# Where the x tiles begin in a partition, and when the first sum of w_out's blocks takes its temporaries

## The chip, the core and the metric

The kernel runs on one core of a Trainium2 chip. The metric is the time of one execution on the device, in microseconds (us), as the median of several runs. TensorE (PE) does the matrix products, VectorE (DVE), ScalarE (ACT) and GpSimd (POOL) the work between them, and SyncE (SP) issues the transfers (DMA). Each engine takes its instructions in a fixed order and waits, where it must, with all that is queued behind.

## What is computed

Attention with a window of keys and block summaries, then a feed-forward layer whose activation is the square of relu:

```python
def _attn_ref(q, k, v):                       # (4, 8, 768, 64) each
    block, window = (32, 16)
    k_sum = k.reshape(B, H, nb, block, D).max(axis=3)
    v_sum = v.reshape(B, H, nb, block, D).mean(axis=3)
    scores_l = scale * np.matmul(q, k.transpose(0, 1, 3, 2))
    mask_l = np.abs(pos[:, None] - pos[None, :]) < window
    scores_s = scale * np.einsum('bhsd,bhnd->bhsn', q, k_sum) + np.log(block)
    scores_all = np.concatenate([np.where(mask_l, scores_l, -1e9), scores_s], axis=-1)
    a = softmax(scores_all)
    return np.matmul(a, np.concatenate([v, v_sum], axis=2))

def _moe_ref(x, w_in, w_out):                 # x: 3072 x 512, the attention's result
    h = x @ w_in                              # 512 x 2048
    g = np.maximum(h, 0.0) ** 2
    return g @ w_out                          # 2048 x 512
```

## The kernel before

**Tiling.** The 3072 tokens are six units of 512. A group is 64 tokens; eight groups make a unit. For each group the kernel forms scores against 118 keys (94 of the window and 24 blocks), a softmax, and the values, and writes the result x into two SBUF tiles: `xh`, x rounded to the engine's fast 32-bit type, and `xl`, the rest. Both are rings of two units (16 groups x 64 tokens x 4 slices of 128). Weights and activations are split in the same way, and each product is made of three terms (high by high, high by low, low by high).

**Products.** `FI{u}_{f}` is the first product of unit u with block f of w_in (16 blocks): 12 matmuls of 128x512, eight that stream `xh` and four that stream `xl`, on L1018 for units 0 and 1 and on L1305 for the later ones. `FO{u}_{f}` is the second product, 12 matmuls on L1042 that stream w_out. For the last four units the second products are taken on sums of blocks (a two-level scheme that spares products): L1419 has 112 groups of six matmuls (`FP`), that stream sums of w_out's blocks; a mixed stage near 440 to 522 us does a part of the first products in the same way (`SP0`, `SP1`, ..., L1610), with sums of x in `xs`, `xgh`, `xgl`, `xa`, or in `xkb`, which are parts of the tile `kb` that is free by then.

**Weights.** Block f of w_in and of w_out comes as 64-bit words (`WL0_f` and `WL1_f`, two loads of 512 KB on SP, L952). It is converted by a chain over two engines: ACT forms `t` from `raw` (`WM`, L955), DVE shifts `raw` (`WR`, L958) and joins the two (`WJ`, L964), ACT rounds to the high part of `w` (`WH`, L969), DVE forms the low part (`WW`, L972). `t` is one of three temporaries, which the sums below take too.

**Sums of w_out's blocks.** `combine(p)` adds two blocks of w_out on POOL (`RC`, L1111, and `SC`, L1126), rounds on ACT (`SH`, L1129), forms the rest on DVE (`SL`, L1132), and stores sums (`WS`) and plain blocks (`WA`, L1144, three transfers of 256 KB) in DRAM, from where they are fetched for the later products.

**Values.** The probabilities of a group are transposed by a turn through DRAM: `TW` stores them (four transfers of 64 KB, L826), `TR` fetches them (256 KB, L832). The visit `V{g}` on PE is the scores of two later groups (L638) and then the values of the groups g-1 and g (L842), which wait for `TR`.

**Order.** A planner in the kernel sets the order on each engine before anything is built. Every task has a due time, worked out from constants (`Q_LEAD`, `AT_FIRST`, `KEEPS`, `PRODUCT_STEP` and others), a modelled duration, and lists of what it waits for and what buffers it takes (`take`) and uses (`use`); `behind` names a task that must have begun before. The planner gives an engine the ready task with the earliest due time.

**Addresses.** Constant tiles (`cst.tile`) lie one behind the other in each partition, in the order in which they are made. `LINE` is 256 bytes. `scratch` and the three `nm` tiles are 64 bytes each; before, none of them lies ahead of `xh`, and in the program as built `xh` begins 1664 bytes into the partition, `xl` at 18048 and `kb` at 47488: each 128 bytes past a multiple of 256. The tiles of weights, activations and sums other than `xkb` begin at multiples of 256.

Of the kernel before, what the change touches and what calls it, by code (L numbers as in the profile page):

```python
# [10 lines left out]
F32 = mybir.dt.float32  # L11
# [9 lines left out]
P = 128  # L21
# [5 lines left out]
LINE = 256  # L27
# [3 lines left out]
TU = UG * TQ  # L31
# [18 lines left out]
FV_LEAD = 0  # L50
FV1_LEAD = 17.0
HALVED = 2
Q_LEAD = 23
XS_LEAD = 7
R_LEAD = 1
TR_LEAD = 18
WITH_ITEM = 0, 0, 1, 1, 0, 1, 0, 0, 0, 1, 0, 0, 1, 1, 1, 1
AT_FIRST = 3
LATER = 22
EARLIER = 12  # L60
X_LEAD = 0
KEEPS = 20
GH_LEAD = 9


# [172 lines left out]
def attention_then_relu2_ffn(  # L238
# [13 lines left out]
    NT, DM = out.shape  # L252
# [14 lines left out]
    cst = ctx.enter_context(tc.tile_pool(name="cst", bufs=1))  # L267
# [4 lines left out]
    add = plan.add  # L272

    kinds = {}
# [3 lines left out]
    def const(shape, name, dtype=F32):  # L278
        cols = -(-4 * math.prod(shape[1:]) // LINE) * LINE // 4
        return cst.tile([shape[0], cols], dtype, name=name)[:, : math.prod(shape[1:])]  # L280
# [54 lines left out]
    MIXED_STEP = 1.66  # L335
    X_BY = 40
    SUMS = 231.1, 245.7, 260.4, 275.0
    PRODUCT_STEP = 1.48, 1.58, 1.40
    A0, A1, B0, B1 = 12.0, 2.0, 21.0, 2.2
    HALF_AT = 25.0, 32.0  # L340
    MX = 0.95
# [1 line left out]
    unit_at, products_at, at = [], [], T0  # L343
# [31 lines left out]


    ident = cst.tile([P, P], F32, name="ident")
    kb = sb.tile([P, NPAIR, NB + S], F32, tag="kb", name="kb", bufs=1)
    xh = cst.tile([P, KT, RING * TQ], F32R, name="xh")
    xl = cst.tile([P, KT, RING * TQ], F32R, name="xl")  # L380
# [34 lines left out]
            )  # L415


    scratch = cst.tile([P, LINE // 16], F32, name="scratch")
    kinds["nm"] = Slots(None, "nm", 3, [cst.tile([P, LINE // 16], F32, name=f"nm{i}") for i in range(3)])

    def table():
        nc.scalar.activation(scratch[:, :1], unscale[:, :1], AF.Exp)
# [25 lines left out]
    for g in reversed(range(NG)):  # L448
        pairs = (P, NPAIR, P)
# [32 lines left out]
    vs_bufs = {}  # L482

    means = const([P, S // P * NB], "means")

    def make_means():

# [200 lines left out]
    def softmax(g, by_pe=False):  # L688
# [104 lines left out]
        if wide:  # L793
            at_ps = h_buf(f"t{g}")

            def turn():
                for p in range(NPAIR):
                    nc.tensor.transpose(
                        out=at_ps.tile[:, p * P : (p + 1) * P], in_=pr.tile[:, p, :], identity=ident
                    )  # L800

            t_T[g] = add(f"T{g}", "PE", 0.5, turn, due - 9, [t_n, t_ident], take=[at_ps], use=[pr])

            def turned():
                nc.scalar.copy(
                    out=a.tile.rearrange("k (i n r) -> k n i r", i=NSQ, n=NPAIR),
                    in_=at_ps.tile.rearrange("k (n i r) -> k n i r", n=NPAIR, i=NSQ),
                )

            t_A[g] = add(f"A{g}", "ACT", 0.47, turned, due - 8.5, [t_T[g]], take=[] if early else [a], use=[at_ps] + [a] * early)  # L810
        else:


            def turn():
                nc.vector.transpose(
                    out=a.tile.rearrange("p (j n r) -> p j n r", j=NSQ, n=NPAIR),
                    in_=pr.tile.rearrange("p n (j c) -> p j n c", c=SQ),
                )

            assert not early  # L820
            t_T[g] = add(f"T{g}", "DVE", 0.63, turn, due - 9, [t_n], take=[a], use=[pr])
            d = buf("turn", 4, (NSQ, SQ, NSQ, NPAIR * SQ), F32, f"turn{g}", dr)

            def store():
                for i in range(NSQ):
                    nc.sync.dma_start(  # L826
                        out=d.tile[:, :, i, :].rearrange("j c e -> c j e"),
                        in_=a.tile[i * SQ : (i + 1) * SQ].rearrange("c (j e) -> c j e", j=NSQ),
                    )

            def fetch():
                nc.sync.dma_start(out=a.tile, in_=d.tile.rearrange("j c i e -> (j c) (i e)"))  # L832

            t_w = add(f"TW{g}", "SP", 1.75, store, due - 8.5 - TR_LEAD, [t_T[g]], take=[d], use=[a], size=4 * P * DM)
            t_A[g] = add(f"TR{g}", "SP", 0.35, fetch, due - 8 - TR_LEAD, [t_w], use=[a, d], size=4 * P * DM)

    def values(both, x_of):
        for i, g in enumerate(both):
# [78 lines left out]


    t_W = {}
    w_parts = {}  # L920

    def convert(f, ns):

# [53 lines left out]
        for i in range(k):  # L977
# [2 lines left out]
                behind=t1[0] if i else None, size=P * 4096, begin=due - 31,  # L980
            ))
        t2 = add(f"WM{name}", "ACT", 0.02 + 0.5 * k, rebias, due - 8, t1, take=[t], use=[raw])
        t3 = add(f"WR{name}", "DVE", 0.09 + 0.27 * k, rest, due - 8, t1, use=[raw])
        t4 = add(f"WJ{name}", "DVE", 0.03 + 0.54 * k, join, due - 7, [t2, t3], use=[raw, t])
        t6 = add(f"WH{name}", "ACT", 0.08 + 0.43 * k, high, due - 6, [t4], take=[w], use=[t])
# [116 lines left out]

    def combine(p):

        due = unit_at[0] + 75 + 13.5 * p + LATER * (p > 5)
        ws = [w_parts[1, 2 * p + k] for k in range(2)]
        raw = buf("t", 3, (P, 2 * DM), F32, f"cr{p}")
        sums = buf("t", 3, (P, 2 * DM), F32, f"cs{p}")
# [38 lines left out]
        for k in range(2):  # L1147
            t1.append(add(
                f"RC{p}_{k}", "POOL", 1.3, lambda k=k: whole(k), due + 1.3 * k, t_W[1, 2 * p + k],
                take=[raw, sums] * (not k), use=[raw] * k + ws[k], begin=due, behind=t1[0] if k else None,  # L1150
            ))
        t2 = add(f"SC{p}", "POOL", 2.9, add_up, due + 2.6, t1, use=[raw, sums])
        t3 = add(f"SH{p}", "ACT", 0.97, high, due + 6, [t2], use=[raw, sums])
# [308 lines left out]
    def sum_x():  # L1462
# [10 lines left out]
            tag: [buf(tag, n, (P, DM), F32R, f"x{tag}{k}") for k in range(2)] for tag, n in (("a", 2), ("gl", 3), ("gh", 3))  # L1473
        }

        def halves(x, k0=0):
            return [Part(x, (2 * k0 + k) * TU, (2 * k0 + k + 1) * TU) for k in range(2)]

        homes = {
            3: (halves(of_kb), halves(of_kb, 1)), 0: (halves(of_kb, 2), pairs["a"]), 2: (halves(slots[0]), pairs["gl"]),  # L1480
            1: (halves(slots[1]), pairs["gh"]),
        }
        takes = {
# [373 lines left out]
```

## Time and profile before

| what | us |
|---|---|
| timed runs | 599.33, 600.30, 601.23 |
| median of the runs | 600.3 |
| the profiled execution | 604.56 |
| span of its trace | 602.7 |
| PE busy in the span | 585.3 (97%) |
| DVE busy | 415.9 (69%) |
| ACT busy | 342.2 (57%) |
| POOL busy | 96.6 (16%) |

The span runs from the first to the last instruction of the profiled execution; 1.9 us of that execution lie around it. The profiled execution is 4.26 us longer than the median of the timed runs. Starts in a timeline are microseconds from the span's start. Matmuls are pipelined: a matmul's own duration reaches over the start of the next, so that the pace of PE is read from start to start.

### The profile page before, as it was taken

How to read it: one execution, taken by the hardware profiler on the slowest of the kernel's cores; microseconds unless marked ns; L12 is line 12 of the kernel's file. 1: busy time of each engine (PE TensorE's matmuls, PEld its weight loads, DVE VectorE, ACT ScalarE, POOL GpSimd, SP SyncE). 2: the span in 40 equal slices, each digit the busy share in tenths (PEclk: the TensorE clock that was granted, in tenths of full speed). 3: DMA queues.
4: the chain of work that ended last, by engine and by line, in shares of the span. 5: the costliest groups of instructions: out<-in, count | busy, mean ns of one | idle time of the engine just before them, and what ended most of it. 6: DMA issues, size and time to landing. Idle time of an engine off the chain costs nothing.

```text
span 602.7 us, 11842 instructions
## 1 busy us (share of the span) xinstructions
PE 585.3 (97%) x4108; PEld 473.5 (79%) x4108; DVE 415.9 (69%) x942; ACT 342.2 (57%) x848; POOL 96.6 (16%) x141
## 2 busy tenths in 40 slices
PE   8889999989999999999989999999999999999996
PEld 6678878768887888888877888888888878788885
DVE  5999897666544615655975867798754945678764
ACT  2899687566654535564864566645643544454442
POOL 4400005263450016264300000000000000000000
PEclk9999999989999999999999999999999999999999
DMA  8999964977994757966998765878976144567672
GB/s 312 294 386 327 346 247 156 299 253 234 380 326 152 237 197 230 358 221 231 283 306 283 227 185 179 278 226 239 312 216 191 35 145 151 161 194 226 193 228 100
DMA packets 100958, 143.83 MB, mean 239 GB/s; under 512 B 10060, under 2 KB 55116, under 8 KB 100900
## 3 DMA queue, kind: packets, MB, share of 16 engines
q1 hardware_dynamic: 100900, 143.09, 73.3%
q8 instruction: 32, 0.52, 0.4%
q14 instruction: 26, 0.21, 0.1%
HBM read 102.42 MB, written 39.85 MB: 236 GB/s over the span
## 4 chain that ended last, share of the span: by engine, by line
PE 82%; DMA 7%; DVE 5%; ACT 2%; issue 2%; SPq 1%; DVEq 0%
PE o L1419 25%; PE h L1305 22%; PE o L1042 10%; PE h L1018 9%; PE o L1610 4%; PE x L842 3%; PE att L638 2%; DMA a<-turn 2%; PE sz L1610 2%; PE o L638 1%; DVE t L964 1%; DMA q<-qW 1%; DMA kb<-kT 1%; PE att L1610 1%; DMA v<-vS 1%
## 5 line engine op out<-in xcount | busy, mean ns | idle before, releaser
L1419 PE MATMUL o<-gh,w 128*128 128x512 f32 x448 | 121.0, 391 | 0.0
L1401 ACT CAST gh<-g 128x512 fp32r<-128x512 f32 x112 | 68.5, 621 | 60.9 <-PE o L1419 29.2
L1305 PE MATMUL h<-xh,w 128*128 128x512 f32 x320 | 100.7, 396 | 0.0
L1419 PEld LDWEIGHTS o<-gh,w 128*128 128x128 f32 x448 | 83.6, 188 | 17.8
L1406 DVE TENSOR_TENSOR gl<-g,gh 128x512 fp32r<-128x512 f32 x112 | 77.7, 706 | 24.0 <-ACT gh L1401 23.3
L1018 PE MATMUL h<-xh,w 128*128 128x512 f32 x240 | 76.9, 400 | 1.7 <-DVE w L972 1.0
L1305 PEld LDWEIGHTS h<-xh,w 128*128 128x128 f32 x320 | 59.8, 188 | 14.1
L1315 ACT ACTIVATE r<-h 128x512 f32<-128x512 f32 x48 | 28.5, 596 | 73.8 <-PE h L1305 72.9
L1419 PE MATMUL o<-gl,w 128*128 128x512 f32 x224 | 69.2, 389 | 0.0
L1305 PE MATMUL h<-xl,w 128*128 128x512 f32 x160 | 63.2, 395 | 0.0
L767 ACT ACTIVATE p<-p,nm 128x118 f32<-128x118 f32 x160 | 61.2, 388 | 2.5 <-DVE nm L712 2.5
L1042 PE MATMUL o<-w,gh 128*128 128x512 f32 x240 | 62.5, 396 | 0.0
L1018 PEld LDWEIGHTS h<-xh,w 128*128 128x128 f32 x240 | 45.3, 190 | 13.3 <-DVE w L972 1.7
L1042 PEld LDWEIGHTS o<-w,gh 128*128 128x128 f32 x240 | 44.9, 190 | 10.4
L1419 PEld LDWEIGHTS o<-gl,w 128*128 128x128 f32 x224 | 42.0, 188 | 9.0
L1018 PE MATMUL h<-xl,w 128*128 128x512 f32 x120 | 47.9, 400 | 0.0
L1032 DVE TENSOR_TENSOR gl<-r,gh 128x512 fp32r<-128x512 f32 x30 | 22.9, 764 | 33.6 <-PE o L1042 21.8
L712 DVE CUSTOM_DVE_ANT_0 p<-att,mask 128x118 f32<-128x118 f32 x152 | 32.9, 274 | 13.6 <-PE att L638 13.5
L651 POOL COPY kb<-kb 128x96 f32<-128x96 f32 x25 | 11.0, 440 | 181.2 <-ACT kw L663 60.4
L1111 POOL TENSOR_TENSOR cr<-w 128x512 f32<-128x512 f32 x16 | 26.4, 1666 | 73.3 <-PE vps L539 41.5
L1027 ACT ACTIVATE r<-h 128x512 f32<-128x512 f32 x30 | 17.9, 597 | 32.5 <-PE h L1018 32.5
L1305 PEld LDWEIGHTS h<-xl,w 128*128 128x128 f32 x160 | 30.1, 188 | 7.2
(200 smaller groups left out, 998.4 us busy)
## 6 DMA issues: line engine op xcount, KB each, us to landing
raw<-wW SPq DMA_DIRECT2D x32, 512.0 KB, 7.6
w<-scr_s SPq DMA_DIRECT2D x64, 256.0 KB, 2.8
w<-scr_a SPq DMA_DIRECT2D x48, 256.0 KB, 3.3
turn<-a SPq DMA_DIRECT2D x160, 64.0 KB, 2.6
a<-turn SPq DMA_DIRECT2D x40, 256.0 KB, 4.7
w<-scr_i SPq DMA_DIRECT2D x40, 256.0 KB, 5.5
v<-vS SPq DMA_DIRECT2D x33, 192.0 KB, 6.1
kb<-kT SPq DMA_DIRECT2D x16, 384.0 KB
```

Source lines behind the costliest of these rows:

```text
L712: nc.vector.tensor_tensor_reduce(out=pr.tile[:, j, :KEYS], in0=score_at(g, 0, j), in1=mask_of(g)[0], scale=-SCALE, scalar=-NEG, op0=ALU.ad ...
L767: nc.scalar.activation(x, score_tile(g, p % parts)[:, p] if by_pe else x, AF.Exp, bias=nm.tile[:, p : p + 1], scale=SCALE if by_pe else -1 ...
L1018: nc.tensor.matmul(cut(h), lhsT=lhs.tile[:, k * P : (k + 1) * P], rhs=rhs[:, k, c0 : c0 + n], start=(i == 0), stop=(i == 3 * KT - 1),)
L1032: lambda: nc.vector.tensor_tensor(out=cut(gl), in0=cut(r), in1=cut(gh).bitcast(F32), op=ALU.subtract),
L1042: nc.tensor.matmul(o_of(o, t), lhsT=terms[i][0].tile[:, (t - t0) * P : (t - t0 + 1) * P], rhs=terms[i][1].tile, start=(first and i == 0), ...
L1111: nc.gpsimd.tensor_tensor(out=raw.tile[:, k * DM : (k + 1) * DM], in0=ws[k][0].tile.bitcast(F32), in1=ws[k][1].tile.bitcast(F32), op=ALU.add)
L1305: nc.tensor.matmul(h.tile, lhsT=lhs.tile[:, k * P : (k + 1) * P], rhs=rhs[:, k, c0 : c0 + TU], start=(i == 0), stop=(i == 3 * KT - 1),)
L1315: t2 = add(f"RL{name}", "ACT", 0.56, lambda: nc.scalar.activation(r.tile, h.tile, AF.Relu), due + 2 - R_LEAD, [t1], take=[r], use=[h])
L1401: f"GH{s}_{n}", "ACT", 0.54, lambda x=x, gh=gh: nc.scalar.copy(out=gh.tile, in_=x.tile), due - GH_LEAD, ready,
L1406: lambda x=x, gh=gh, gl=gl: nc.vector.tensor_tensor(out=gl.tile, in0=x.tile, in1=gh.tile.bitcast(F32), op=ALU.subtract),
L1419: nc.tensor.matmul(o.tile[:, d], lhsT=chunk.tile[:, w * HALF + d * P : w * HALF + (d + 1) * P], rhs=y.tile, start=begins and w == 0 and y ...
L1610: nc.tensor.matmul(o.tile, lhsT=lhs(w, k), rhs=y[k], start=begins and i == 0, stop=i == 5, skip_group_check=not begins,)
```

## The change

It has three parts.

1. `scratch` and one `nm` tile are made ahead of `kb`, `xh` and `xl`, and the two other `nm` tiles behind `means`. In the program as built `xh` then begins at 1792 and `xl` at 18176, both multiples of 256; masks, `v`, the probabilities `p` and `means` move by 128 bytes as well, to multiples of 256. `kb` stays at 47488, and the parts of it that hold sums of x (`xkb`) begin 128 bytes further in.
2. The first task of `combine` (`RC0_0`) gets `behind=t_WM[-1]`: it takes its temporaries once the last conversion's `WM15` has begun.
3. Constants of the planner: `Q_LEAD` 23 to 9, `AT_FIRST` 3 to 4, `KEEPS` 20 to 30, the second `PRODUCT_STEP` 1.58 to 1.59, and `combine` due 1 us later. `FETCH_LATE` is zero and has no effect.

```diff
-Q_LEAD = 23
+FETCH_LATE = 0.0
+LATE_FROM = 8
+COMB0 = 76
+COMB1 = 13.5
+Q_LEAD = 9
...
-AT_FIRST = 3
+AT_FIRST = 4
...
-KEEPS = 20
+KEEPS = 30
...
-    PRODUCT_STEP = 1.48, 1.58, 1.40
+    PRODUCT_STEP = 1.48, 1.59, 1.40
...
     ident = cst.tile([P, P], F32, name="ident")
+    scratch, *small = (cst.tile([P, LINE // 16], F32, name=f"small{i}") for i in range(2))
     kb = sb.tile([P, NPAIR, NB + S], F32, tag="kb", name="kb", bufs=1)
     xh = cst.tile([P, KT, RING * TQ], F32R, name="xh")
...
-    scratch = cst.tile([P, LINE // 16], F32, name="scratch")
-    kinds["nm"] = Slots(None, "nm", 3, [cst.tile([P, LINE // 16], F32, name=f"nm{i}") for i in range(3)])
+    kinds["nm"] = Slots(None, "nm", 3, small)
...
     means = const([P, S // P * NB], "means")
+    small += [cst.tile([P, LINE // 16], F32, name=f"small{i}") for i in range(2, 4)]
...
-    w_parts = {}
+    w_parts, t_WM = {}, []
...
         t2 = add(f"WM{name}", "ACT", 0.02 + 0.5 * k, rebias, due - 8, t1, take=[t], use=[raw])
+        t_WM.append(t2)
...
-        due = unit_at[0] + 75 + 13.5 * p + LATER * (p > 5)
+        due = unit_at[0] + COMB0 + COMB1 * p + LATER * (p > 5)
...
-                take=[raw, sums] * (not k), use=[raw] * k + ws[k], begin=due, behind=t1[0] if k else None,
+                take=[raw, sums] * (not k), use=[raw] * k + ws[k], begin=due, behind=t1[0] if k else t_WM[-1],
...
-        def halves(x, k0=0):
-            return [Part(x, (2 * k0 + k) * TU, (2 * k0 + k + 1) * TU) for k in range(2)]
+        def halves(x, k0=0, at=0):
+            return [Part(x, at + (2 * k0 + k) * TU, at + (2 * k0 + k + 1) * TU) for k in range(2)]
...
-            3: (halves(of_kb), halves(of_kb, 1)), 0: (halves(of_kb, 2), pairs["a"]), 2: (halves(slots[0]), pairs["gl"]),
+            3: (halves(of_kb, 0, LINE // 8), halves(of_kb, 1, LINE // 8)), 0: (halves(of_kb, 2, LINE // 8), pairs["a"]), 2: (halves(slots[0]), pairs["gl"]),
```

The planner's order changes with it. The names below are those of the tiles, with a running number behind; lines of the changed kernel are a few higher than those of the kernel before.

**ACT near the end of unit 0, 105 to 130 us.** `r0_10` is the activation of `FI0_10`, `t15<-raw15` is `WM15`, `w15<-t15` is `WH15`, `cr0<-cs0` is `SH0`. Before:

```order
L1027 ACTIVATE r0_10_1451<-h0_10_1425 128x512
...
L955 ACTIVATE t14_1513<-raw14_1467 128x1024
...
L1129 CAST cr0_1496<-cs0_1497 128x1024
...
L1027 ACTIVATE r0_13_1642<-h0_13_1582 128x512
L1028 ACTIVATE r0_13_1642<-r0_13_1642 128x512
L1029 CAST gh0_13_1666<-r0_13_1642 128x512
L955 ACTIVATE t15_1673<-raw15_1423 128x1024
L1027 ACTIVATE r0_14_1696<-h0_14_1653 128x512
L969 CAST w15_1705<-t15_1673 128x2x512
```

And now:

```order
L1033 ACTIVATE r0_10_1452<-h0_10_1426 128x512
L960 ACTIVATE t15_1468<-raw15_1406 128x1024
L1034 ACTIVATE r0_10_1452<-r0_10_1452 128x512
L1035 CAST gh0_10_1475<-r0_10_1452 128x512
L1033 ACTIVATE r0_11_1480<-h0_11_1454 128x512
L974 CAST w15_1495<-t15_1468 128x2x512
...
L960 ACTIVATE t14_1526<-raw14_1470 128x1024
...
L1135 CAST cr0_1518<-cs0_1519 128x1024
L1034 ACTIVATE r0_13_1587<-r0_13_1587 128x512
```

The conversion of block 15 moved from behind the activation of `FI0_13` to the activation of `FI0_10`, ahead of block 14. The two DVE steps of block 15 moved with it, from behind `GL0_13` to around `GL0_10`. PE's own order changes there too: from `FO0_10 FI0_12 FO0_11 V13 FI0_13 FO0_12 FI0_14 FO0_13 FI0_15` to `FI0_12 FO0_10 FI0_13 V13 FO0_11 FI0_14 FO0_12 FI0_15 FO0_13`.

**SP, 97 to 110 us.** `raw15` is loaded by `WL0_15` and `WL1_15`, `scr_a0` by `WA0`, `turn13<-a13` is `TW13` and `a13<-turn13` is `TR13`. Before:

```order
L1144 DMA scr_a0_96<-w1_0_702 256x1x256
...
L952 DMA raw15_1423<-wW 128x512
L826 DMA turn12_1439<-a12_1415 32x4x128 x4
L826 DMA turn13_1446<-a13_1444 32x4x128 x4
L952 DMA raw14_1467<-wW 128x512 x2
L952 DMA raw15_1423<-wW 128x512
L832 DMA a12_1415<-turn12_1439 128x512
L832 DMA a13_1444<-turn13_1446 128x512
```

And now:

```order
L957 DMA raw15_1406<-wW 128x512
...
L957 DMA raw15_1406<-wW 128x512
...
L1150 DMA scr_a0_96<-w1_0_702 256x1x256
L1150 DMA scr_a0_96<-w1_1_745 256x1x256 x2
L831 DMA turn12_1440<-a12_1416 32x4x128 x4
L831 DMA turn13_1447<-a13_1445 32x4x128 x4
L957 DMA raw14_1470<-wW 128x512 x2
L837 DMA a12_1416<-turn12_1440 128x512
```

Both loads of block 15 moved ahead of `WA0`; between the stores and the fetches of the turn stand now two weight loads where there were three.

**PE in the mixed stage, 486 to 492 us.** `o0` is an accumulator whose two halves `SP11` (`xkb`), `SP12` (`xs1`, `xgh`) and `SP13` (`xs0`, `xgl`) write in turn; `h5_13` is that of `FI5_13`. Before:

```order
L1610 MATMUL o0_66<-xkb_5367,w5_948 128x512 x6
L1610 MATMUL o0_66<-xs1_5433,w0_1_665 128x512 x4
L1610 MATMUL o0_66<-xgh0_5437,w0_1_665 128x512
L1610 MATMUL o0_66<-xgh1_5447,w0_1_665 128x512
L1610 MATMUL o0_66<-xs0_5407,w7_1035 128x512 x4
```

And now:

```order
L1616 MATMUL o0_66<-xkb_5367,w6_971 128x512 x6
L1616 MATMUL o0_66<-xs1_5433,w0_1_665 128x512 x4
L1616 MATMUL o0_66<-xgh0_5437,w0_1_665 128x512
L1616 MATMUL o0_66<-xgh1_5448,w0_1_665 128x512
L1311 MATMUL h5_13_5479<-xh_74,w7_1035 128x512 x2
...
L1616 MATMUL o0_66<-xs0_5407,w4_913 128x512 x4
```

`FI5_13`, which came after `SP15`, moved between `SP12` and `SP13`.

## Rows read from the trace of the kernel before

**Rows 1.** The page: busy time, share of the span, instructions of PE.

```profile
PE 585.3 (97%) x4108; PEld 473.5 (79%) x4108; DVE 415.9 (69%) x942; ACT 342.2 (57%) x848; POOL 96.6 (16%) x141
```

**Rows 2.** Waits of PE: who waits for whom; us in total, times, longest.

```profile
PE x L842 <- DMA a<-turn: 1.7, 2, 1.2
PE o L1610 <- ACT g L1628: 1.4, 2, 0.7
PE h L1018 <- DVE w L972: 1.0, 2, 0.8
PE h L1018 <- ACT w L969: 0.7, 1, 0.7
```

**Rows 3.** Groups by line and form: count | busy us, mean ns | idle before.

```profile
L1419 PE MATMUL o<-gh,w 128*128 128x512 f32 x448 | 121.0, 391 | 0.0
L1305 PE MATMUL h<-xh,w 128*128 128x512 f32 x320 | 100.7, 396 | 0.0
L1018 PE MATMUL h<-xh,w 128*128 128x512 f32 x240 | 76.9, 400 | 1.7 <-DVE w L972 1.0 <-ACT w L969 0.7
```

**Rows 4.** Timeline of PE, three places: start, us, line, operation, count, idle before.

```profile
187.06 0.62 PE L1018 MATMUL h<-xh,w 128*128 128x512 f32 x2
...
189.85 1.99 PE L1042 MATMUL o<-w,gh 128*128 128x512 f32 x8
...
192.59 0.62 PE L1018 MATMUL h<-xh,w 128*128 128x512 f32 x2
...
523.17 1.08 PE L1419 MATMUL o<-gh,w 128*128 128x512 f32 x4
...
596.63 0.61 PE L1419 MATMUL o<-gh,w 128*128 128x512 f32 x2
```

**Rows 5.** Timeline of PE in the mixed stage, two places.

```profile
480.61 1.56 PE L1610 MATMUL o<-xkb,w 128*128 128x512 f32 x6
482.01 0.40 PE L1305 MATMUL h<-xh,w 128*128 128x512 f32 x1
...
488.96 1.07 PE L1610 MATMUL o<-xs,w 128*128 128x512 f32 x4
489.87 0.61 PE L1610 MATMUL o<-xgh,w 128*128 128x512 f32 x2
```

**Rows 6.** Timeline of PE at the end of unit 0.

```profile
114.29 1.32 PE L842 MATMUL x<-a,v 118*64 118x64 f32 x32 [1.21 <-DMA a<-turn]
...
125.80 1.07 PE L1042 MATMUL o<-w,gl 128*128 128x512 f32 x4
...
135.98 0.64 PE L638 MATMUL att<-kb,q 64*64 64x118 f32 x16
```

**Rows 7.** Stretches: busy of PE, PEld, DVE, ACT, POOL; granted clock, DMA share, GB/s.

```profile
94.00:98.00 4.00, 4.00 (x19) 3.32 (x18) 3.62 (x16) 3.94 (x17) 2.69 (x4) 1.00 0.27 88
...
108.00:116.00 8.00, 6.79 (x84) 5.39 (x84) 4.00 (x5) 4.82 (x7) 0.16 (x1) 1.00 1.02 330
...
130.00:133.00 3.00, 3.00 (x9) 2.39 (x8) 1.70 (x1) 0.03 (x1) 3.00 (x3) 0.52 0.95 347
```

**Rows 8.** Timeline of SP's DMA issues at the end of unit 0.

```profile
101.34 0.51 SPq L952 DMA_DIRECT2D raw<-wW  x1
101.96 3.82 SPq L826 DMA_DIRECT2D turn<-a  x8
105.83 1.41 SPq L952 DMA_DIRECT2D raw<-wW  x3
107.28 1.08 SPq L832 DMA_DIRECT2D a<-turn  x2
...
128.25 1.14 SPq L832 DMA_DIRECT2D a<-turn  x2
```

**Rows 9.** Timeline of ACT at the end of unit 0.

```profile
110.99 1.17 ACT L955 ACTIVATE t<-raw 128x1024 f32<-128x1024 f32 x1 [5.20 <-DMA raw<-wW]
...
123.66 1.15 ACT L955 ACTIVATE t<-raw 128x1024 f32<-128x1024 f32 x1
```

More of the change, by code (lines that the diff above doesn't have):

```diff
@@ L834, in softmax @@
             t_w = add(f"TW{g}", "SP", 1.75, store, due - 8.5 - TR_LEAD, [t_T[g]], take=[d], use=[a], size=4 * P * DM)
-            t_A[g] = add(f"TR{g}", "SP", 0.35, fetch, due - 8 - TR_LEAD, [t_w], use=[a, d], size=4 * P * DM)
+            t_A[g] = add(f"TR{g}", "SP", 0.35, fetch, due - 8 - TR_LEAD, [t_w], use=[a, d], size=4 * P * DM, late=FETCH_LATE * (g >= LATE_FROM))
     def values(both, x_of):
```

## The prediction

> **What bounds the kernel now.** I read the page's busy times first: PE is busy for 585.3 of 602.7 us [rows 1]. So a saving has to come out of PE: out of its pace while it is busy, or out of its few waits. The other engines, at 69% and less, matter only where PE waits for them. Next the list of PE's waits [rows 2]: four of its entries lie, all but a part of the first, where the order is changed, and they make 4.8 us together. Third, the groups by line, for what a busy PE pays per matmul [rows 3]: those that stream `xh` (L1018, L1305) average 396 to 400 ns, the L1419 ones, of the same shape, 391. Such a duration overlaps the next, so the real pace is read from starts. `FI` at 187.06 to 189.85 makes 12 matmuls in 2.79 us, 232.5 ns each; the `FO` behind it, 189.85 to 192.59, 12 in 2.74; and from 523.17 to 596.63 lie 324 matmuls of L1419, 226.7 ns each [rows 4]. Whatever streams x is 2.6% slower per matmul than whatever streams w or sums of w.
>
> Is that the address? The mixed stage compares on one line, into the same accumulators, with the same kind of weights: six that stream `xkb`, 480.61 to 482.01, take 233 ns each; four that stream `xs`, 488.96 to 489.87, 227.5 [rows 5]. `xkb`, `xh` and `xl` begin 128 bytes past a multiple of 256, `xs` on one. What the matmul writes, and which product it is, is thus no explanation; the place of the streamed operand is, though a trace of before can't exclude another property that these three tiles share.
>
> **Part 1, the addresses.** Per matmul 232.5 - 226.7 = 5.8 ns. `FI` matmuls: L1018 has 240 with `xh` [rows 3], at eight of twelve per product 30 products; L1305 has 320 [rows 3], 40 products, and by the code eight more with weights in other tiles. That makes 78 products and 936 matmuls; the mixed stage adds 112 that stream `xh`, `xl` or `xkb`. 1048 x 5.8 ns = 6.1 us. The product behind an `FI` seems to pay a little too, 2.74 against 12 x 0.2267 = 2.72, some 15 to 20 ns; for 30 `FO`s and some 20 places in the mixed stage 0.8 us. Ceiling 6.9. Not all of it reaches the end: up to the ninth product of unit 0 PE follows the conversions on DVE, and two visits (near 200 and 324 us) wait for a transfer that doesn't start earlier; I take off 0.7. **6.2 us**, with bounds: nothing if the address is not the cause, 6.9 if all reaches the end. `v`, the weights of the 640 value products, moves to a multiple of 256 too. No row shows `v` in either place, so its price lies between nothing and, at the same 5.8 ns for each, 3.7 us; weight loads run beside matmuls here (PEld 79% busy under PE's 97% [rows 1]), so I take nothing and keep the other end for the range. Masks, `p` and `means` are operands of engines with room: nothing either way.
>
> A page speaks against this part. The Trainium skill, "SBUF — State Buffer", section "Specifications (TRN2)", gives cachelines of 16 bytes and names no larger unit; 128 and 256 are both whole numbers of them, so by that rule a shift of 128 bytes moves no matmul. Rows 5 don't agree with that being all; the case has its rival below.
>
> **Part 2, the last conversion.** `FI0_15` waits twice, for `WH15` on ACT and then `WW15` on DVE, 0.7 and 0.8 us [rows 2]. The cause is on ACT: `WM15` begins at 123.66, behind the softmax of groups 14 and 15 and `GH0_13` [rows 9], though half of its weights were asked for at 101.34 and the rest before 107.3 [rows 8]. And it costs more than the waits: from 130 to 133 us the granted clock is 0.52 [rows 7], the lower of the two levels (1.2 instead of 2.4 GHz), right behind PE's pauses. Sum by starts: from 125.80, where the last four matmuls of a product begin, to 135.98, where the next visit does, stand 4 + 12 + 12 matmuls [rows 6]; at 227, 233 and 227 ns they need 0.91 + 2.79 + 2.72 = 6.42 of the 10.18 us. 3.76 are lost; some 1.7 of that to the clock (6 matmuls of `FI0_15` and those of `FO0_14` at up to twice the time), 2.0 to the waits and to PE's refill. In the new order `WM15` stands behind the activation of `FI0_10`, some 18 us earlier, and both loads of block 15 ahead of `WA0`, so the wait goes whole: **3.7 us**, or 2.0 if the timed runs don't show the lower clock that this execution shows. The first sum gives its place up: `RC0` waits for `WM15`, and `SC0` for the temporary that `WW15` frees, on POOL, where nobody on PE waits for it; behind it on the queues stand `SH0` (ACT) and `SL0` (DVE), and behind those the softmax of groups 14 and 15. That is the rival on V15.
>
> **Part 3, V13.** It waits 1.21 us for the fetch of the turned probabilities [rows 2, 6]. The fetches are issued at 107.28, right behind three weight loads of 512 KB issued from 105.83 [rows 8], and the transfers run full from 108 to 116 us at 330 GB/s [rows 7], while from 94 to 98 us they were 0.27 busy. One of the three now goes out near 100 us: 512 KB / 330 GB/s = 1.6 us earlier landing, near 112.7. PE, by a faster x, is there near 112.4 instead of 113.1, with as many products before it as before. Wait 0.3 instead of 1.2: **0.9 us**; bounds 0 (the place is taken by other transfers) and 1.2.
>
> **Then V15.** Where a wait goes, the next need comes sooner. The fetch for V15 was issued at 128.25 to 129.4 [rows 8], and its values begin one microsecond behind 135.98 [rows 6]: ample. With part 2, part 3 and x, PE is there some 5.5 us earlier, near 131.4. The fetch hangs on DVE and ACT (softmax of groups 14, 15), which get only part of that, so it lands between 129 and 133. I take **0.7 us given back**, bounds 0 and 1.6.
>
> **Mixed stage.** `SP13` waits 0.7 us for ACT to copy half of its accumulator [rows 2], one of two waits of that kind. With `FI5_13` (2.8 us) in front the copy is covered: **0.8 us** with the refill, bounds 0 and 1.0. The second wait stands between products whose order is unchanged and stays. The other constants swap loads late in the kernel, ahead of which PE has no wait in the list; q's loads go out later, but no entry of PE's waits names them: nothing, up to 1 us lost.
>
> **Sum.** -6.2 - 3.7 - 0.9 + 0.7 - 0.8 = -10.9 us on the profiled execution of 604.56 us: 593.7. That execution is 4.26 us above the median of the timed runs; from 600.3 the same sum gives 589.4, and 591.1 without the clock's share. I set **590.0**.
>
> **The rivals.**
> (a) The address is not the cause. Then all matmuls on x stay at 233 ns, and 600.3 - 4.7 = 595.6. For it: three tiles only share an address class, and the page above. Against: rows 5, on one line. 0.10.
> (b) The address works, the end of unit 0 gives its gain back, because V15 waits for its fetch longer than I took or the clock falls behind that new pause. 600.3 - 6.2 - 0.8 - 0.9 = 592.4. For it: the fetch's chain runs over three engines and SP. Against: the wait begins only if the fetch lands after 131.4. 0.22.
> (c) Slower. `WM15` now stands on ACT in front of `SQ0_10` and `GH0_10`. If block 15's weights land late, ACT stands with all of that behind it, and so does PE at `FO0_10`. In before a load issued at 105.83 kept ACT waiting till 110.99, 5.2 us [rows 8, 9]; both loads of block 15 are issued by about 102, so by 107 they are there. PE reaches `FO0_10` some 5.6 us after `FI0_10`'s end, of which ACT and DVE need 3.6, so it loses one us for each that the weights land after 107.8, and to be over 602.1 with the rest of the sum right they must land after 120.5 (after 114.3 if (a) holds too). Time then 603 or more. Against: SP issues them ahead of `WA0`. 0.04.
> (d) The gain is larger: `v` counts too. 600.3 - 10.9 - 2 to 3.7 = 586 to 587. 0.04.
>
> **How the numbers follow.** Forecast 0.60, (a) 0.10, (b) 0.22, (c) 0.04, (d) 0.04. The range goes from 586.5 (forecast with most of what `v` could give) to 595.0 (all of (b) and the lower half of (a)); about 0.1 is left out above and little below. What a measurement of this kernel can tell from no change is about 0.3%, 1.8 us. Faster by more than that: forecast, (b), (d) and most of (a), 0.93. Within: 0.03, a mixture of (a) and a partial (c). Slower: 0.04.
>
> **What would show it.** In the changed kernel's trace: L1018's and L1305's matmuls at the pace of L1419 (12 in about 2.72 us, means near 391 ns); if they stay at 2.79, part 1 is wrong. `FI0_15` without a wait, and a granted clock of 1.00 from 130 to 134 us; else part 2. PE's wait for `a<-turn` at V13 under 0.5 us, and at V15 under 1; else part 3 or (b). One wait for L1628's copy instead of two. A wait of ACT for `raw` longer than 2 us before `WM15` would be (c). The prediction is wrong if a new wait over 2 us stands in PE's list, or if the streams of x keep their pace.

## The result and the profile after

| | before | after |
|---|---|---|
| median of seven runs each, us | 601.23 (599.27 to 604.92) | 595.08 (593.83 to 598.31) |
| the profiled execution | 604.56 | 595.08 |
| span of its trace | 602.7 | 593.0 |
| PE busy in the span | 585.3 | 577.6 |

The ratio after to before is 0.9894 (95% interval 0.986 to 0.9928): a gain of 6.2 us where 10.3 were forecast. The time lies 0.08 us above the upper end of the range; as a gain, from 600.3, the range went from 5.3 to 13.8 us, and 6.2 lies in it. The two traces differ by 9.7 us; but the profiled execution of before was 3.3 us above the median of its seven runs and that of after is its median, and 9.7 - 3.3 = 6.4.

The groups by line and form of after (count | busy us, mean ns of one | idle before), which answer to [rows 3]:

```profile
L1425 PE MATMUL o<-gh,w 128*128 128x512 f32 x448 | 120.6, 391 | 0.0
L1311 PE MATMUL h<-xh,w 128*128 128x512 f32 x320 | 99.1, 391 | 0.0
L1024 PE MATMUL h<-xh,w 128*128 128x512 f32 x240 | 74.2, 390 | 0.0
```

And the timeline of PE at the place of [rows 4]:

```profile
184.42 0.62 PE L1024 MATMUL h<-xh,w 128*128 128x512 f32 x2
...
187.14 1.98 PE L1048 MATMUL o<-w,gh 128*128 128x512 f32 x8
...
189.86 0.39 PE L1024 MATMUL h<-xh,w 128*128 128x512 f32 x1
```

The streams of x now have the mean of the others, and an `FI` takes 2.72 us, 226.7 ns a matmul, as does the `FO` behind it. Part 1 does what it says. The list of PE's waits (us in total, times, longest), against [rows 2]:

```profile
PE x L847 <- DMA a<-turn: 3.7, 3, 1.8
...
PE o L1616 <- ACT g L1634: 0.7, 1, 0.7
```

No wait of an `FI` for ACT or DVE is left in it, and one of the two waits in the mixed stage is gone; the wait for fetched probabilities has grown from 1.7 to 3.7 us. The timeline of PE shows where (in brackets the idle time before, and what ended it):

```profile
130.03 0.63 PE L643 MATMUL att<-kb,q 64*64 64x118 f32 x16
...
132.91 0.69 PE L847 MATMUL x<-a,v 118*64 118x64 f32 x16 [1.84 <-DMA a<-turn]
...
133.90 0.82 PE L847 MATMUL x<-a,v 118*64 118x64 f32 x16 [0.30 <-DMA a<-turn]
...
138.91 0.39 PE L1024 MATMUL h<-xh,w 128*128 128x512 f32 x1
```

The row at 130.03 is the start of V15, that at 138.91 the start of `FI1_0`. V13 waits no longer, V15 does, and behind that wait the clock falls: stretches of after (length, then busy of PE, PEld, DVE, ACT, POOL, granted clock, DMA share, GB/s), against [rows 7]:

```profile
126.00:130.00 4.00, 4.00 (x19) 3.05 (x17) 4.00 (x3) 1.39 (x3) 2.32 (x2) 1.00 0.54 166
130.00:134.00 4.00, 1.85 (x52) 1.52 (x53) 0.90 (x9) 0.00 (x0) 0.00 (x0) 1.00 1.03 332
134.00:138.00 4.00, 4.00 (x25) 3.20 (x24) 1.87 (x10) 3.24 (x14) 1.23 (x2) 0.57 1.08 388
```

In before it was at the lower of its two levels from 130 to 133 us, behind the pauses of `FI0_15`; now it is from 134 to 138, behind that of V15.

Where the 9.7 us arise, by the starts of tasks that both traces have:

| start of | before | after | lead of after |
|---|---|---|---|
| `FI0_10` | 98.09 | 97.12 | 0.97 |
| V13 | 112.04 | 111.14 | 0.90 |
| V15 | 135.98 | 130.03 | 5.95 |
| `FI1_0` | 140.92 | 138.91 | 2.01 |
| `FI2_0` | 234.47 | 231.21 | 3.26 |
| V31 | 302.42 | 297.96 | 4.46 |
| V35 | 345.50 | 339.66 | 5.84 |
| `SP12` | 488.96 | 481.18 | 7.78 |
| first of the last `FP` stage | 521.78 | 512.07 | 9.71 |

Between V13 and V15 the edit gains 5.05 us; between V15 and `FI1_0`, where nothing was edited, 3.94 are lost again. From the start of V15 to that of `FO0_15` it is 4.62 us in after and 2.05 in before: 2.14 of waiting, and 0.43 in which PE starts anew behind its two pauses. `FO0_15` itself takes 4.26 us instead of 2.89: 1.37 for the lower clock. After that the lead only grows.

### The profile page after: what moved, and what is told of

Read it like the earlier page. It is cut to its first block, busy times and chain, and to the rows that moved or that the text cites. A ratio compares the mean times of both kernels' runs of the same rounds, so it can differ in the third digit from the quotient of the medians.

```text
span 593.0 us, 11845 instructions
## 1 busy us (share of the span) xinstructions
PE 577.6 (97%) x4108; PEld 473.5 (80%) x4108; DVE 414.4 (70%) x942; ACT 342.2 (58%) x848; POOL 92.2 (16%) x141
## 4 chain that ended last, share of the span: by engine, by line
PE 74%; DMA 15%; DVE 4%; SPq 3%; issue 2%; ACT 1%; DVEq 0%; ACTq 0%
PE o L1425 24%; PE h L1311 22%; PE o L1048 8%; PE h L1024 7%; DMA raw<-wW 4%; PE o L1616 4%; PE x L847 3%; PE att L643 2%; DMA a<-turn 2%; PE sz L1616 2%; DMA v<-vF 1%; DMA turn<-a 1%; DMA qvpa_lent<-vF 1%; DMA kb<-kT 1%; DMA scr_a<-w 1%
## 5 line engine op out<-in xcount | busy, mean ns | idle before, releaser
L1311 PE MATMUL h<-xh,w 128*128 128x512 f32 x320 | 99.1, 391 | 0.0
L1024 PE MATMUL h<-xh,w 128*128 128x512 f32 x240 | 74.2, 390 | 0.0
L1311 PE MATMUL h<-xl,w 128*128 128x512 f32 x160 | 62.3, 389 | 0.0
L772 ACT ACTIVATE p<-p,small 128x118 f32<-128x118 f32 x160 | 61.1, 386 | 1.3 <-DVE small L717 1.3
L1024 PE MATMUL h<-xl,w 128*128 128x512 f32 x120 | 46.7, 389 | 0.0
L656 POOL COPY kb<-kb 128x96 f32<-128x96 f32 x25 | 9.5, 378 | 178.2 <-ACT kw L668 59.6
L1117 POOL TENSOR_TENSOR cr<-w 128x512 f32<-128x512 f32 x16 | 25.0, 1584 | 59.5 <-PE vps L544 40.7
```

Source lines behind the costliest of these rows:

```text
L772: nc.scalar.activation(x, score_tile(g, p % parts)[:, p] if by_pe else x, AF.Exp, bias=nm.tile[:, p : p + 1], scale=SCALE if by_pe else -1 ...
L1024: nc.tensor.matmul(cut(h), lhsT=lhs.tile[:, k * P : (k + 1) * P], rhs=rhs[:, k, c0 : c0 + n], start=(i == 0), stop=(i == 3 * KT - 1),)
L1117: nc.gpsimd.tensor_tensor(out=raw.tile[:, k * DM : (k + 1) * DM], in0=ws[k][0].tile.bitcast(F32), in1=ws[k][1].tile.bitcast(F32), op=ALU.add)
L1311: nc.tensor.matmul(h.tile, lhsT=lhs.tile[:, k * P : (k + 1) * P], rhs=rhs[:, k, c0 : c0 + TU], start=(i == 0), stop=(i == 3 * KT - 1),)
```

## The experiments

Ratios are to the kernel before on the same chip, with 95% intervals. Four runs stand first: the addresses alone, the order alone, the kernel before once more, and one fetch put ahead of a store.

**The addresses alone.** The kernel before with

```diff
+    scratch, *small = (cst.tile([P, LINE // 16], F32, name=f"small{i}") for i in range(2))
     kb = sb.tile(...)
     xh = cst.tile(...)
...
-            3: (halves(of_kb), halves(of_kb, 1)), 0: (halves(of_kb, 2), pairs["a"]), ...
+            3: (halves(of_kb, 0, LINE // 8), halves(of_kb, 1, LINE // 8)), 0: (halves(of_kb, 2, LINE // 8), pairs["a"]), ...
```

> The kernel before with the new addresses alone (xh, xl, xkb at multiples of 256; order of every engine as before). Theory A, the address sets the pace of the matmuls that stream x: 12 of an FI in 2.72 us instead of 2.79, 6 to 7 us less in all, ratio 0.988 to 0.990; the waits at V13 and FI0_15 stay or grow by what PE gains ahead of them. Rival B, the pace comes with the order or with something else of the changed kernel: FI stays at 2.79 us, ratio 1.00.

Measured: 597.26 us, ratio 0.9927 (0.9898 to 0.9955), span 595.7. Its groups by line and form:

```profile
L1306 PE MATMUL h<-xh,w 128*128 128x512 f32 x320 | 99.3, 391 | 0.0
L1019 PE MATMUL h<-xh,w 128*128 128x512 f32 x240 | 74.7, 392 | 2.2 <-ACT w L970 1.0 <-DVE w L973 0.8 <-ACT r L1028 0.4
```

The pace is there with the old order, and the waits of `FI0_15` stay. Some 70% of the gain, 4.4 us, comes from the addresses.

**The order alone.** The changed kernel with the four small tiles behind the x tiles again, and `LINE // 8` set to 0.

> The changed kernel with the old addresses (xh, xl, xkb 128 bytes past a multiple of 256; order as in the changed kernel). If the new order gives its gain at FI0_15 back at V15, as the trace of the changed kernel shows (a wait of 2.1 us there, and the lower clock behind it), the order is worth 1 to 3 us: V13's wait and the mixed stage's; ratio 0.995 to 0.999, FI at 2.79 us. If the order is what made the changed kernel faster, ratio near 0.99.

Measured: 601.45, ratio 0.9999 (0.9968 to 1.0031). The streams of x are back at the old pace, PE waits at V15, and there is a wait that neither kernel has:

```profile
L1310 PE MATMUL h<-xh,w 128*128 128x512 f32 x320 | 100.7, 396 | 0.0
```

```profile
PE x L846 <- DMA a<-turn: 4.0, 4, 1.8
...
PE o L1047 <- ACT gh L1034: 1.8, 1, 1.8
```

On ACT that last one looks like this, and from 106 to 111 us the granted clock is 0.67:

```profile
104.66 1.17 ACT L959 ACTIVATE t<-raw 128x1024 f32<-128x1024 f32 x1 [4.34 <-DMA turn<-a]
```

ACT stands 4.34 us in front of `WM15`, and `FO0_10` with it: the mechanism of rival (c). The row names a transfer of the turn, which shares a semaphore of the queue with the load that ACT needs; the second half of block 15 landed at 104.58 here and at 103.00 in after. In after ACT stands there 2.45 us, until 103.09, and `FO0_10` is just in time. So the order gains at `FI0_15` and V13, gives it back at `FO0_10` and V15, and comes out at nothing. Alone the two parts gave 4.4 and 0.1 us, together 6.2. The 1.8 us between lie within the intervals; the wait at `FO0_10`, which after doesn't have, would account for them, but one trace of each doesn't settle that.

**The kernel before once more**, as a second label in the same comparison.

> The kernel before once more, unchanged, for a second trace. Its first profiled execution took 604.56 us, its timed runs 599.3 to 604.9. If executions differ by what happens at the end of unit 0 (the clock's fall behind FI0_15's waits, V13), this trace shows another length of the stretch from 98 to 141 us with the rest of the span alike; if they differ at the start (loads of the first groups), the stretch from 0 to 45 us differs. Median 600 to 601.

Measured: 603.47, ratio 1.0034 (1.0004 to 1.0065). Two copies of one program can thus stand 0.3% apart; differences below that carry nothing here. Its trace shows the clock at 0.51 from 36 to 43 us, 0.77 from 303 to 308, and 1.00 over the end of unit 0:

```profile
36.00:43.00 7.00, 6.54 (x42) 6.43 (x43) 6.56 (x22) 5.92 (x22) 0.00 (x0) 0.51 1.04 399
120.00:140.00 20.00, 18.75 (x135) 14.70 (x134) 14.36 (x44) 13.00 (x35) 12.37 (x11) 1.00 0.74 245
303.00:308.00 5.00, 3.82 (x36) 3.09 (x33) 1.52 (x10) 2.75 (x12) 0.00 (x0) 0.77 1.01 328
```

The lower clock of 130 to 133 us [rows 7] is thus not in every execution of the old order. Of its five traces here, before shows it, and the one with `xh` at 192 below (0.72 from 128 to 134 us); this one, the addresses alone and the one with `xh` at 32 don't, though `FI0_15` waits 1.25 to 1.78 us in each of them.

**One store behind the fetch.** In after, three stores of w_out's blocks (`WA2`) are issued on SP from 127.81 and the fetches for V15 only at 129.72. Here the planner's order list is edited, as in all runs that follow:

```diff
+MOVED = (("WA2", "TR15"),)
...
+        for name, behind in MOVED:
+            tasks.remove(named[name])
+            tasks.insert(tasks.index(named[behind]) + 1, named[name])
```

> The changed kernel with one step of SP moved: the three stores of WA2 (768 KB) come behind the fetches TR14 and TR15 instead of ahead of them. Theory: V15's wait of 2.1 us is the fetch's place behind WA2; TR15 is issued 1.9 us earlier and lands near 131 instead of 133.8 us, V15 waits under 0.5 us, the granted clock stays at 1.00 from 134 to 138 us, and 2 to 4 us are won against the changed kernel: some 591.5 to 593 where that has 595. Rival: the transfers ahead (the fetch's own 512 KB, WS0) are what holds it; then the wait stays at 2 us and the time at 595.

Measured: 595.51, ratio 0.991 (0.9882 to 0.9938), not to be told from after. The timeline of PE:

```profile
131.59 0.69 PE L848 MATMUL x<-a,v 118*64 118x64 f32 x16 [1.05 <-DMA a<-turn]
...
150.02 0.73 PE L1049 MATMUL o<-w,gh 128*128 128x512 f32 x2 [2.56 <-ACT os L1086]
```

V15 waits 1.05 us instead of 2.14, and the clock stays at 1.00 from 128 to 136 us, as expected; the wait itself was expected under 0.5. But the stores land later, a temporary comes free later, and 2.56 us are lost in unit 1. The wait has moved.

**Other addresses.** Small tiles ahead of `xh` and between `xh` and `xl` put the two at other offsets past a multiple of 256 bytes, in the order of before: one look each.

> The order of the kernel before, xh beginning 192 bytes and xl 64 bytes past a multiple of 256. Start to start of the matmuls that stream x, in a row of an FI. If only a multiple of 256 gives the pace of 226.7 ns, both run at 231 to 234 ns on average, as at 128. If a multiple of 64 is enough, both run at 226.7, and 128 must be slow for another reason, which would speak against theory A.

> The order of the kernel before, xh beginning 32 bytes and xl 160 bytes past a multiple of 256. If the start has to be a multiple of 256, the pace is 231 to 234 ns on average, perhaps with another pattern from matmul to matmul; if the cost grows with finer misplacement, it is over 234; if only 128 is bad, 226.7.

The first has `xh` at 192 and `xl` at 64, the second 32 and 160:

```profile
L1307 PE MATMUL h<-xh,w 128*128 128x512 f32 x320 | 100.5, 395 | 0.0
...
L1307 PE MATMUL h<-xl,w 128*128 128x512 f32 x160 | 62.5, 391 | 0.0
```

```profile
L1307 PE MATMUL h<-xh,w 128*128 128x512 f32 x320 | 99.5, 392 | 0.0
...
L1307 PE MATMUL h<-xl,w 128*128 128x512 f32 x160 | 63.2, 395 | 0.0
```

Two products, start to start, in the first of them:

```profile
269.42 0.63 PE L1307 MATMUL h<-xh,host 128*128 128x512 f32 x2
...
272.19 0.63 PE L1307 MATMUL h<-xh,host 128*128 128x512 f32 x2
...
274.98 0.62 PE L1307 MATMUL h<-xh,w 128*128 128x512 f32 x2
```

A product takes 2.77 and 2.79 us here. In the second it takes 2.75 from 237.85 on and 2.80 twice from 267.12 on, against 2.72 with both tiles at 0 and 2.79 to 2.80 with both at 128: neither pair of offsets gives the pace of 0, and 2.75 us, 229 ns a matmul, is below the 231 to 234 that were expected. In the built program of the second run the tiles behind, `w`, `gh` and `gl` among them, lie 32 bytes further on too. Streams of these keep their pace: an `FO`, which streams `w`, takes 2.72 us (235.13 to 237.85), and six matmuls of `FP` take 1.36 (540.18 to 541.54), 226.7 ns each. So 32 bytes cost these streams nothing. One look gives no verdict on the time (605.14 and 599.71 us); the pace is what they were run for.

**More stores, and the conversion later on its engines.** On top of after, eight store tasks, four of plain blocks of w_out (`WA`) and four of blocks of w_in (`WK`), go behind the fetches for V19 and V21; in the second run `WM15` also goes behind `GH0_10` on ACT and the DVE steps of block 15 behind `GL0_10`:

```diff
+MOVED = (("WA2", "TR19"), ("WA3", "WA2"), ("WK10", "WA3"), ("WK11", "WK10"),
+         ("WA4", "TR21"), ("WA5", "WA4"), ("WK14", "WA5"), ("WK15", "WK14"),
+         ("WM15", "GH0_10"), ("WJ15", "GL0_10"), ("WR15", "GL0_10"))   # second run only
```

> The changed kernel with eight stores that nothing reads before 222 us (WA2, WA3, WK10, WK11 and WA4, WA5, WK14, WK15, 5.2 MB) moved on SP from the stretch 127 to 170 us behind the fetches TR19 and TR21. Theory: from 128 to 176 us the transfers set the pace (DMA share 0.95 to 1.04), so whatever PE gains ahead is given back at the next fetch or store that it needs (V15, then FO1_0_1 behind WS2, V17, V19). Then V15 waits under 0.7 us, FO1_0_1, V17 and V19 don't wait, and 1.5 to 3.5 us are won against the changed kernel. Rival: the fetch's own chain (softmax of groups 14 and 15, transposes, TW15's landing) sets V15; then V15 still waits 1 to 2 us and the time is that of the changed kernel.

> As e6, and WM15 behind the rounding of FI0_10's activation on ACT (with its two DVE steps behind that one's), so that a late landing of block 15's weights doesn't hold PE at FO0_10. Where these weights land late, as in the trace of the new order with the old addresses (1.8 us of PE at FO0_10), the wait goes; in executions where they land early nothing changes. 0 to 1.5 us below e6, none of PE's waits at FO0_10.

Measured: 593.60, ratio 0.9889 (0.984 to 0.9939), and 593.09, 0.9888 (0.9848 to 0.9927). The wait in unit 1 is gone. V15 still waits, in two pieces, 0.58 + 1.23 = 1.81 us in the first and 2.00 in the second:

```profile
132.56 0.69 PE L851 MATMUL x<-a,v 118*64 118x64 f32 x16 [0.58 <-issue]
...
134.47 0.69 PE L851 MATMUL x<-a,v 118*64 118x64 f32 x16 [1.23 <-DMA a<-turn]
```

The expectation for the first run was under 0.7; its rival, that the fetch's own chain sets V15, is what came. The second trace shows what is then the longest single wait, at V31:

```profile
300.36 0.39 PE L852 MATMUL x<-a,v 118*64 118x64 f32 x4 [1.90 <-DMA a<-turn]
```

From 300 to 307 us its clock is 0.54. Neither run can be told from after by its time.

**What pins V15.** In after the softmax of groups 14 and 15 starts on DVE at 118.66, in before at 118.52: PE is six microseconds earlier at V15, DVE not at all. The trace's chain of work there (start, us, engine, tile, line):

```profile
110.88 1.19 ACT t L960
...
112.72 1.22 DVE t L969
...
115.52 0.95 ACT cr L1135
...
116.49 2.25 DVE cs L1138
118.73 0.19 DVE p L717
...
120.93 0.60 DVE gl L1038
...
125.27 0.72 DVE a L820
```

It hangs on the landing of block 14's weights near 110.8, which is as late as in before. The last transpose for V15 (the row at 125.27) even begins 1.76 us later than in before, and with it the stores of the turn, three stores of w_out's blocks and then the fetch. First before, then after:

```profile
123.51 0.71 DVE L815 STREAM_TRANSPOSE a<-p 128x512 f32<-128x512 f32 x1
...
126.33 1.87 SPq L1144 DMA_DIRECT2D scr_a<-w  x3
```

```profile
127.81 1.86 SPq L1150 DMA_DIRECT2D scr_a<-w  x3
129.72 1.14 SPq L837 DMA_DIRECT2D a<-turn  x2
```

In after a step of `gl` (120.93) stands in between, and steps of the softmax that take 0.65 us in before take 0.87 and 0.93, while POOL adds for most of that time (121.44 to 124.7). So the softmax was taken out from behind `SH0` and `SL0` (the rows on `cr` and `cs` in the chain). The first run below puts it, with what it needs, ahead of `SH0`, `SL0` and `WS0`; the second also puts the third sum (`RC2`, `SC2`, `SH2`, `SL2`, `WS2`) later, so that temporaries are free; the third also moves tasks at V31:

```diff
+    # first: behind WJ14 a chain that ends in ... TW15 TR14 TR15 SQ0_13 GH0_13 GL0_13 SH0 SL0 WS0
+    # second, besides: RC2_0 RC2_1 SC2 SH2 SL2 WS2 behind PC0_3
+    # third, besides:
+    ("CL0_6", "TW30"), ("CL0_8", "TW31"), ("TR30", "CL0_9"), ("TR31", "TR30"),
```

> As e6_stores, and the softmax of groups 14 and 15 (with V15's stores and fetches TW14, TW15, TR14, TR15 on SP) ahead of the low part SL0, the high part SH0 and the stores WS0 of the first sum. Theory: V15's fetch is pinned by DVE: in the kernel before and in the changed one the softmax begins at 118.5 to 118.7 us, behind WW14 and SL0, which hang on the landing of block 14's weights, so no gain of PE reaches it. With the softmax first, T15 ends near 122 instead of 126 us, TR15 lands before 130, V15 doesn't wait; the next limit is FO1_0_1, which waits for WS2's landing near 150 (2 to 3 us). Time 0 to 2 us below e6_stores. Rival: V15 waits for transfers; then TR15 lands near 133 again.

> As e8_softmax, and the third sum of w_out's blocks takes its temporaries behind the copies PC0_2 and PC0_3 of unit 0's output, so that these don't wait for its stores WS2. Theory: FO1_0_1 doesn't wait any more, FI1_0 to V17 keep what PE gained at V15: 3 to 4 us below the changed kernel in the stretch from 98 to 176 us, 590 to 592 us in all. If instead V17 or V19 wait for their fetches, the gain is given back there.

> As e9_temps, and at V31 (near 298 us) TW30 ahead of CL0_6, TW31 ahead of nothing but behind CL0_8's place moved after it, TR30 and TR31 right behind CL0_9: V31's wait of 1.6 to 2.4 us falls under 1, and the clock, which fell to half in three of the traces behind this wait, stays at 1.00 from 300 to 308 us: 1 to 3 us below e9_temps.

Measured: 598.44, ratio 0.9945 (0.9908 to 0.9983); 599.86, 0.9984 (0.9949 to 1.0019); 598.85, 0.996 (0.9928 to 0.9991). All three lie above the store run that they start from (0.9889), so the times that were expected, below it, did not come. No trace of the first can be read against the others, and what it was expected to do to V15 stays open. In the second V15 has no wait, as wanted, but the next product does:

```profile
129.78 1.15 PE L853 MATMUL x<-a,v 118*64 118x64 f32 x32
...
133.91 0.73 PE L1054 MATMUL o<-w,gh 128*128 128x512 f32 x2 [2.97 <-ACT gh L1041]
```

ACT shows why: the rounding of the second sum stands in front and waits for POOL.

```profile
131.63 1.04 ACT L1141 CAST cr<-cs 128x1024 fp32r<-128x1024 f32 x1 [7.55 <-POOL cs L1138]
133.24 0.62 ACT L1041 CAST gh<-r 128x512 fp32r<-128x512 f32 x1
```

POOL in its turn had waited for the temporary that `WS0`, moved later, still held. V15's wait can be removed; what it cost is then paid on ACT, and waits of 1.03, 1.07 and 0.47 us, at 175.88, 177.64 and 197.03, come on top.

**The fastest version.** The edits of the second store run, and the V31 moves:

> As e7_both (the changed kernel with eight stores later and block 15's conversion behind FI0_10's activation), and at V31 the stores and fetches of the turn ahead of loads that are needed later: CL0_6 behind TW30, CL0_8 behind TW31, TR30 and TR31 right behind CL0_9. In e10_v31 the same moves took V31's wait from 2.0 to under 0.1 us. So here V31's wait of 1.9 us goes, and with it the clock's fall behind it: 1.5 to 3 us below e7_both, 590 to 592 us. V15 still waits some 2 us, since nothing here touches its fetch's chain on DVE.

Measured: 590.24 us (589.73 to 591.94), ratio 0.9791 (0.9752 to 0.9831). The interval lies below that of after (0.986 to 0.9928); each is against before on its own chip, and the two were not run side by side. At V31 PE now waits 0.19 us (row 297.82), where after waited 1.58, and the clock there is 1.00; V15 keeps its wait, 0.44 + 1.21 = 1.65 us, and the stretch behind it a mean of 0.83:

```profile
131.88 1.07 PE L853 MATMUL x<-a,v 118*64 118x64 f32 x16 [1.21 <-DMA a<-turn]
...
297.82 0.69 PE L853 MATMUL x<-a,v 118*64 118x64 f32 x16 [0.19 <-DMA a<-turn]
```

```profile
128.00:138.00 10.00, 8.35 (x84) 6.61 (x83) 4.59 (x21) 4.66 (x20) 2.86 (x4) 0.83 0.90 303
296.00:310.00 14.00, 13.81 (x116) 11.51 (x116) 10.26 (x33) 9.28 (x28) 0.00 (x0) 1.00 1.00 321
```

The same V31 moves were worth 1.0 us behind the softmax edits, less than two copies of one program can differ by, and 2.9 here, by medians taken on different chips. That V31's wait can be removed is shown; how much of the difference to after comes from it, and how much from the clock, is not.

## Why the prediction was right and wrong

**Part 1, right in mechanism, and in size as far as the medians tell.** 232.5 ns became 226.7, in each run with x on a multiple of 256 bytes and in no other. That the `FP` matmuls stream sums of w_out, as the kernel's description has it, is not so: they stream `gh` and `gl`, with the sums as weights. These tiles begin at multiples of 256 as well, so the comparison holds. Rival (a) is dead, though its time, 595.6, came closer than the forecast's: a time alone would have confirmed the wrong story, and only the starts in [rows 4] and their counterparts separate the two. The median gave 4.4 us (2.7 to 6.1, from the interval) for the 6.2 taken. Why less is not settled. Each run has a mean granted clock, and it differs between runs of one program (below). Of the runs of before and of the addresses alone on one chip, those with a mean of 0.998 or more have medians of 600.1 (14 of 34 runs) and 593.9 (6 of 12), 6.2 us apart; but the others are 4.0 apart, and the clock's mean over all of them is 0.996 on either side, so the clock doesn't explain the difference. The means of the same runs are 5.2 us apart. In the one trace of each, part of the gain comes back in waits: at V31 the addresses alone wait 2.41 us for transfers and before waits 1.57, at `FI0_15` 1.78 and 1.53, together 1.1 us where the prediction took 0.7 off.

**Rival (d), nothing.** The 640 value products average 225 ns before and 226 after, though `v` moved.

**Part 2, right on the waits, wrong on what they are worth.** `FI0_15` has no wait, and with V13, whose 1.2 us are gone too, the stretch from V13 to V15 gained 5.05 us, where parts 2 and 3 made 4.6 and x adds some 0.3. The failing part is the 1.7 us counted for the clock. Two of the five executions of the old order show that price and three don't, and after has one nearly as large, 1.37 us, behind V15. The edit moved the pause, and where the clock falls behind a pause, its price moved with it. The sign that the prediction gave, a clock of 1.00 from 130 to 134 us, came true all the same: the stretch lies four microseconds later.

**"Then V15", the step that failed.** 0.7 us was taken, with 0 to 1.6 as bounds; it is 2.14 of waiting, 0.43 of starting anew and 1.37 of clock, 3.94; the prediction's own sign against it was a wait over 1 at V15. The prediction let the softmax of groups 14 and 15 get "only part" of PE's 5.5 us. It got none: it is pinned by the landing of block 14's weights through five steps on ACT and DVE, none of which the edit moves. Its fetch is issued at 129.72 instead of 128.25, because its last transpose on DVE begins at 125.27 instead of 123.51 (three stores stand ahead of it in both), and landed at 133.76 instead of 131.95 us. That is rival (b), with a larger price than its own 592.4, which had no clock in it. Its point of decision, a landing after 131.4, was right.

**Rival (c), real and not costly here.** ACT did wait before `WM15`, 2.45 us in after, more than the 2 that the prediction named as its sign. But the threshold of 107.8 took the end of another block's activation for that of `FI0_10`; by the order alone, where ACT stood until 104.66 and `FO0_10` lost 1.8 us, and by after, 103.09 and next to nothing, it lies near 103.

**Mixed stage, undersized.** The order alone gained 1.34 us between `SP12` and the last stage, for the 0.8 taken; that only one of the two waits would go was right.

**Which base.** The sum of 10.9 was made on an execution of 604.56 us and carried by subtraction to 600.3, the median of three runs; that of seven is 601.23, and this alone is 0.9 us of the miss. The longer execution seems to hold more slow stretches than the median one (the time goes with the granted clock, below), and savings read off it are then partly savings of its bad luck. With V15 at 3.94 instead of 0.7 and the mixed stage at 1.34, the same sum gives 10.9 - 3.2 + 0.5 = 8.2 on that execution; the traces show 9.7 (a wait of 0.5 us at V33 is gone too, which no edit was meant for, and the rest, 1.0 us, is not accounted for), the medians 6.2.

## What to carry to other kernels

Read the pace of matmuls from start to start, and compare streams that differ only in where their operand lies: 128 bytes of small tiles moved ahead of large ones gave most of this gain. When an edit lets one engine arrive earlier, follow the next need back to what pins it (here a weight load that did not move) before crediting the lead; a wait that is removed pays only if what stands behind it moves too. And a slow stretch of the clock behind a pause is credited to an edit only if several executions show it at that place.

## What the runs showed of the hardware

**Where a streamed operand begins.** Mean ns of the 128x512 matmuls of one line by the bytes past a multiple of 256 at which the tile begins:

| offset | `xh` | `xl` |
|---|---|---|
| 0 | 391 | 389 |
| 32 | 392 | |
| 64 | | 391 |
| 128 | 396 | 395 |
| 160 | | 395 |
| 192 | 395 | |

Of the offsets tried only 0 for both tiles gave 2.72 us a product. By the means 32 and 64 are near 0, and at 32 the streams of `w`, `gh` and `gl` keep 226.7 ns. The products with x at 32 or 64 take 2.75 to 2.80 us, and there the other tile lies at 160 or 192; what 64 costs alone stays open, and so does why one stretch with `xh` at 32 takes 2.80 and others 2.75. All of these offsets are whole numbers of the 16-byte cachelines that the Trainium skill gives ("SBUF — State Buffer", "Specifications (TRN2)"), so that rule does not explain the difference.

**The clock and the spread of runs.** Of the thirteen traces used here all but two, the addresses alone and that with `xh` at 32, have a slow stretch behind some pause of PE, at varying places. A pause doesn't always bring one: in the new order, of eight traces six have a slow stretch (0.57 to 0.72) within 132 to 142 us, behind the wait of V15 or the one that took its place, and two don't. Over all runs of before in these comparisons (86) the time falls by about 7 us for each 0.01 that the mean granted clock is higher, from 607.89 at 0.988 to between 598.9 and 601.3 at 1.0. The spread of one program goes with the clock; how much of it the clock makes and how much the pauses ahead of it is not separated. The fastest version runs at 0.996 to 1.0 and spreads over 2.2 us, where after spreads over 4.5 at 0.995 to 0.997; but the third softmax run, whose V31 wait is removed too, spreads over 5.9.

**DVE beside POOL.** The same step of a sum on DVE, 128x1024, took 2.25 us at 116.49 in after, while POOL added from 116.36 on, and 1.21 us with POOL idle in the first store run. First after, then the store run:

```profile
116.36 3.53 POOL L1117 TENSOR_TENSOR cr<-w 128x512 f32<-128x512 f32 x2 [4.11 <-DVE w L977]
```

```profile
128.79 1.21 DVE L1142 TENSOR_TENSOR cs<-cs,cr 128x1024 fp32r<-128x1024 f32 x1
```

The Trainium skill, "SBUF — State Buffer", "Who interferes with whom", says that a DVE instruction with two inputs in SBUF contends with a GpSimd instruction that reads there; the trace agrees, with a factor of 1.9. In this kernel DVE's chain to the next fetch pays for a sum that POOL makes.
